# Output projection: the tail rows held in both row halves, with a ScalarE copy of the second tile's tail

## The chip, the cores and the metric

The kernel runs on one core of a Trainium2 chip. The metric is the time of one execution in microseconds of device time. A smaller number is better.

## The reference

Four layers are applied in turn to `x` of shape 1 x 2048 x 576: attention, gated unit, attention, gated unit. Each adds to `x` and starts with a layer norm. Both attention layers use the same weights, and so do both gated units.

```python
def _A_ref(x, wqkv, wo):                     # H = 32 heads of Dh = 18
    qkv = transpose((x @ wqkv).reshape(B, S, 3, H, Dh), 2, 0, 3, 1, 4)
    q, k, v = qkv[0], qkv[1], qkv[2]
    idx = pos[:, None] - (arange(8) * 2)[None, :]      # 8 positions, 2 apart
    ...
    attn = softmax(where(idx >= 0, q . kg * Dh ** -0.5, -1e9))
    o = sum over the window of attn * vg
    return o.transpose(0, 2, 1, 3).reshape(B, S, D) @ wo

def _B_ref(x, w_gate, w_up, w_down):         # F = 4608
    return ((x @ w_gate) * (x @ w_up)) @ w_down

x = x + _A_ref(_layernorm(x), A_wqkv, A_wo)
x = x + _B_ref(_layernorm(x), B_w_gate, B_w_up, B_w_down)
x = x + _A_ref(_layernorm(x), A_wqkv, A_wo)
x = x + _B_ref(_layernorm(x), B_w_gate, B_w_up, B_w_down)
```

The last step of the attention, `o @ wo`, is the output projection. The change is there.

## The kernel before, in words

The 2048 rows are cut into tiles of 128. A block `j` is an attention layer and a gated unit over one or two tiles (`nst` is 1 or 2). The first four blocks have one tile, the other 14 have two.

The width of 576 is four pieces of 128 (`KF` = 4) and a tail of 64 (`TL`). The attention keeps its result transposed in `oT`: 128 partitions, five pieces (the fifth, index `KF`, is the tail), and up to 256 columns, which are the rows of the block, 128 for each tile. In the tail piece the lower 64 partitions hold zeros. VectorE forms `oT` as a sum of eight products over the window (the first product at L772, the adds at L786). `wo_p` holds the weights in the same layout. Its tail fills partitions 0 to 63 (two DMAs, L392), and a memset on GpSimd (L341, part of `mk_zero`) puts zeros into partitions 64 to 127.

In blocks of one tile, the projection uses the whole array: five matmuls with 128 rows for each half of the output columns (L826).

In blocks of two tiles, the array is used as two halves of 64 rows which work side by side. `strip(i, r, hh, first)` is the list of matmuls of tile `i` on row half `r` (0 is partitions 0 to 63, 1 is 64 to 127) for output column half `hh` (288 columns). Row half 0 goes over five pieces and row half 1 over four, since the tail is only in the upper partitions. A tile's two column halves are summed in two PSUM banks, one of the `pg` and one of the `pu` family (`acct` and `pa` are the fourth of each). In a first pass half 0 works on the bank of the first column half while half 1 works on the other; in a second pass they swap. The order is: tile 0 first pass, tile 1 first pass, tile 0 second pass, tile 1 second pass. `both(a, b, fence)` issues two such lists in alternation, one matmul of each at a time. `fence` (L471) makes ScalarE copy one element, `tok`, from a bank when the tile's first pass is done; the first matmul of the second pass waits for that copy. When both passes are done, VectorE adds each bank to `xf` (`res`, L796), and this frees the bank.

The other users of TensorE in this scheme are `quarter` (L900, gate and up projections), `down2` (L968 and L969, down projection) and `project` (L527, query, key and value). They split their work over the two row halves in the same way, and their own tails are held for both halves.

The order of the work on each engine is not written out by hand. `Plan` is a planner that runs when the program is built: each `op` names an engine, an expected cost in ns, what it reads (`r`) and writes (`w`), and a priority. The planner gives each engine a list of instructions by its own estimate of start times, and the engines then go through these lists in order. An `op` may have a `margin`, which is added to the time when its inputs are ready: for the projection that is 500 ns in block 4 and 5 and 1200 ns after. The `tok` copies, the evacuations of gated units (L911 on ScalarE, L912 on VectorE) and `res` are marked as due, which puts them ahead of attention work that would delay them. So another cost or another dependence can change the order on every engine.

At the start, SP issues the loads in this order: rows of `x` and the query, key and value weights, then `wo_p`, then the gated unit's weights in six slices, with the first slabs of `w_down` between them.

Of the kernel before, what the change touches and what calls it, by code (L numbers as in the profile page):

```python
# [10 lines left out]
ACT = mybir.ActivationFunctionType  # L11
# [21 lines left out]
class Plan:  # L33
# [13 lines left out]
    def op(self, eng, cost, fn, r=(), w=(), prio=1, after=None, hold=None, free=None, margin=0, nbytes=0, use=None,  # L47
           pair=None, need=None, due=False, late=0, half=False):
        o = Op()
        o.rank, o.late, o.half = -1 if due else self.rank, late, half  # L50
        o.eng, o.cost, o.fn, o.prio, o.hold, o.free = eng, cost, fn, prio, hold, free
        o.margin, o.idx, o.succ, o.order, o.nbytes = margin, len(self.ops), [], set(), nbytes
        o.lat, o.use, o.pair, o.need = self.LAT[eng], use, pair, need
        d = set()
        for k in r:
            d.update(self.wr.get(k, ()))
        for k in w:
            d.update(self.wr.get(k, ()))
# [12 lines left out]
        o.n = len(d | o.order)  # L71
        self.ops.append(o)
        return o
# [96 lines left out]
def kernel(  # L170
# [12 lines left out]
    nc = tc.nc  # L183
    _, S, D = A_x.shape
    F = B_w_gate.shape[1]
    P = 128
    H, W, DIL = 32, 8, 2
    Dh = D // H
    HALO = (W - 1) * DIL
    KF = D // P  # L190
    TL = D - KF * P
    KT = KF + 1
# [6 lines left out]
    HD = D // 2  # L199
# [22 lines left out]
    wo_p = sb("wo_p", [P, KT, D])  # L222
# [21 lines left out]
    oT = sb("oT", [P, KT, CH])  # L244
    n_al = nlayers // 2
# [47 lines left out]
    def dma(dst, src):  # L293
        return lambda: nc.sync.dma_start(dst, src)
# [36 lines left out]
    def setup_b():  # L331
        def mk_zero():
            for t_ in qT_:
                nc.gpsimd.memset(t_[TL:P, KF, :], 0.0)
            for t_ in kv_:
                nc.gpsimd.memset(t_[TL:P, :, KF, :], 0.0)
            nc.gpsimd.memset(q_x[TL:P, KF, :], 0.0)
            nc.gpsimd.memset(kv_x[TL:P, :, KF, :], 0.0)
            for t_ in halo:
                nc.gpsimd.memset(t_[:], 0.0)  # L340
            nc.gpsimd.memset(wo_p[TL:P, KF, :], 0.0)  # L341
        op("POOL", 2600, mk_zero, w=[f"{x}{t}{i}" for x in "qkv" for t in (4, "H") for i in ZN] + [f"halo{i}" for i in range(n_al)] + ["wo_z"])
        for k in range(KT):
            def perm(eng, cost, key, t3, rk, k=k):
                if t3 < 3:
                    wr = wrawb[:, k, :] if t3 == 2 else wrawa[:, k, t3 * D:(t3 + 1) * D]
                    src = wr.rearrange("p (h d) -> p d h", h=H)[:, 0:16, :]
                    dst = wqkv[:, k, t3 * 512:(t3 + 1) * 512].rearrange("p (d h) -> p d h", h=H)
                else:
                    t0, t1 = (0, 2) if t3 == 3 else (2, 3)  # L350
                    src = (wrawa, wrawb)[t3 - 3][:, k, :].rearrange("p (t h d) -> p t d h", t=t1 - t0, h=H)[:, :, 16:18, :]
                    dst = wqkv[:, k, 3 * 512:3 * D].rearrange("p (t d h) -> p t d h", t=3, h=H)[:, t0:t1]
                fn = {"DVE": nc.vector.tensor_copy, "POOL": nc.gpsimd.tensor_copy, "ACT": nc.scalar.copy}[eng]
                pl.rank = 0.5
                op(eng, cost, lambda: fn(dst, src), r=rk, w=[key], prio=2 + (t3 in (2, 4)))  # L355
                pl.rank = 0
            ra, rb = [[f"wraw{c}{k}"] if k < KF else [f"wrawt{c}0", f"wrawt{c}{TL}"] for c in "ab"]
            perm("DVE", 530, f"wq0_{k}", 0, ra)
            perm("DVE", 180, f"wq3_{k}", 3, ra)
            if k % 2:  # L360
                perm("DVE", 530, f"wq1_{k}", 1, ra)
            else:
                perm("ACT", 1000, f"wq1_{k}", 1, ra)
            perm(VP[k], {"ACT": 1050, "DVE": 560, "POOL": 1250}[VP[k]], f"wq2_{k}", 2, rb)
            perm(VT[k], {"ACT": 330, "DVE": 200, "POOL": 300}[VT[k]], f"wq4_{k}", 4, rb)

        def mk_sel():
            nc.gpsimd.memset(Esel[:], 0.0)
            nc.gpsimd.memset(Bsel[:], 0.0)
            for j in range(4):  # L370
                nc.gpsimd.affine_select(out=Esel[:], in_=Esel[:], compare_op=ALU.not_equal,
                                        fill=1.0, base=-32 * j, pattern=[[-1, 32]], channel_multiplier=1)
                nc.gpsimd.affine_select(out=Bsel[:, j], in_=Bsel[:, j], compare_op=ALU.not_equal, fill=1.0,
                                        base=-32 * j, pattern=[[0, 4], [-1, 32]], channel_multiplier=1)
        op("POOL", 2900, mk_sel, w=["sel"], prio=3)

        def mk_cap():
            nc.gpsimd.memset(cap[:], 3e38)
            for i_ in range(W):
                if wlist[i_] > 0:  # L380
                    nc.gpsimd.memset(cap[:, i_, 0:DIL * wlist[i_]], -1e9)
        op("POOL", 1000, mk_cap, w=["cap"], prio=3.5)

        op("DVE", 0, lambda: None, r=[f"wq{t}_{k}" for t in (0, 1, 3) for k in range(KT)], w=["prod0", "prod1", "s10", "Lt"])
        op("ACT", 0, lambda: None, r=[f"wq{t}_{k}" for t in (2, 4) for k in range(KT)], w=["s11", "s12", "ab"])

    def setup_wo():
        wv_ = A_wo.rearrange("(h d) n -> h d n", d=Dh)
        for dd in range(4):
            op("SP", 470, dma(wo_p[32 * dd:32 * dd + 32, 0:KF, :], wv_[:, dd:16:4, :]), w=[f"wo{dd}"], nbytes=32 * KF * D * 2, prio=2.6)  # L390
        for dd in range(2):
            op("SP", 470, dma(wo_p[32 * dd:32 * dd + 32, KF, :], wv_[:, 16 + dd, :]), w=[f"wot{dd}"], nbytes=32 * D * 2, prio=2.6)  # L392

    def setup_glu():
        fw = F // FS
# [5 lines left out]
            op("SP", 550, dma(wgu_t[0:TL, fs], B_w_gate[KF * P:D, fs]), w=[f"wgt{s}"], nbytes=TL * fw * 2, prio=4 + s)  # L401
            op("SP", 550, dma(wgu_t[TL:2 * TL, fs], B_w_up[KF * P:D, fs]), w=[f"wut{s}"], nbytes=TL * fw * 2, prio=4 + s)

    wok = ["wo_z", "wot0", "wot1"] + [f"wo{dd}" for dd in range(4)]

    def head(src, keys, nst, dst, key, prio, ab, on_pe, mg, c0=0, halves=False):

# [56 lines left out]
    def both(a, b, fence=None):  # L464
        its = [f() for p in zip_longest(a, b) for f in p if f]
        if fence:
            tc.add_manual_dep(its[0].ins, fence["at"].ins.name, sync)

    def fence(box, src, keys):
        def fn():  # L470
            box["at"] = nc.scalar.copy(tok[0:1, :], src())  # L471
        op("ACT", 190, fn, r=keys, prio=0, due=True)
# [20 lines left out]
    def attention(j, la, t0, nst):  # L493
# [20 lines left out]
        def bank(p_, u):  # L514
            return (pg, pu)[p_][u["slot"]]
# [281 lines left out]
        if nst == 2:  # L797
            us = [{"left": 2}, {"left": 2}]
            fs = [{}, {}]
            o = None  # L800

            def strip(i, r, hh, first):
                def one(t):
                    rows = slice(TL * r, TL * r + TL)
                    return nc.tensor.matmul(bank(hh, us[i])[:, 0:HD], lhsT=oT[rows, t, i * P:(i + 1) * P], rhs=wo_p[rows, t, hh * HD:(hh + 1) * HD],  # L805
                                     start=(first and t == 0), stop=(not first and t >= KF - 1), skip_group_check=True)
                return [lambda t=t: one(t) for t in range(KF + 1 - r)]
            for first in (True, False):
                for i in range(nst):
                    kw = dict(pair=tuple(us), margin=mg) if o is None else dict(after=o, need=us[i])  # L810
                    o = op("PE", KT * TILE * HD, lambda i=i, first=first: both(strip(i, 0, 0 if first else 1, first), strip(i, 1, 1 if first else 0, first),
                                                                                           None if first else fs[i]),
                           r=["oT", "oTt", *wok], w=[f"wo{j}_{i}"], prio=0, half=True, **kw)
                    if first:
                        fence(fs[i], lambda i=i: bank(0, us[i])[0:1, 0:1], [f"wo{j}_{i}"])
            for i in range(nst):
                for hh in range(2):
                    op("DVE", 370, lambda i=i, hh=hh: res(bank(hh, us[i]), i, hh), r=[f"wo{j}_{i}", xin_k[i]], w=[fk[i], f"{fk[i]}h{hh}"] + guard,
                       prio=0, free="unit", use=us[i], due=True)
# [291 lines left out]
```

## Time and profile before

| | us |
|---|---|
| median of 3 runs (1056.66 to 1058.14) | 1057.23 |
| the profiled execution | 1056.22 |
| its span, first to last instruction | 1054.4 |
| TensorE busy (99%) | 1040.7 |
| VectorE busy (75%) | 786.2 |
| ScalarE busy (39%) | 410.8 |
| GpSimd busy (1%) | 8.9 |

The span is the part of the profiled execution between its first and its last instruction; 1.8 us lie around it. In the rows of the profile, PE is TensorE's matmuls, PEld its weight loads, DVE is VectorE, ACT is ScalarE, POOL is GpSimd and SP the queue that issues the DMAs. A group of instructions is given by line, engine, operation, output and inputs, shape and count, then busy time and the mean duration of one, then the idle time of the engine ahead of them and what ended it. Matmuls are pipelined, so the duration of one is longer than the distance between two starts.

### The profile page before, as it was taken

How to read it: one execution, taken by the hardware profiler on the slowest of the kernel's cores; microseconds unless marked ns; L12 is line 12 of the kernel's file. 1: busy time of each engine (PE TensorE's matmuls, PEld its weight loads, DVE VectorE, ACT ScalarE, POOL GpSimd, SP SyncE). 2: the span in 40 equal slices, each digit the busy share in tenths (PEclk: the TensorE clock that was granted, in tenths of full speed). 3: DMA queues.
4: the chain of work that ended last, by engine and by line, in shares of the span. 5: the costliest groups of instructions: out<-in, count | busy, mean ns of one | idle time of the engine just before them, and what ended most of it. 6: DMA issues, size and time to landing. Idle time of an engine off the chain costs nothing.

```text
span 1054.4 us, 39972 instructions
## 1 busy us (share of the span) xinstructions
PE 1040.7 (99%) x17845; PEld 829.9 (79%) x17863; DVE 786.2 (75%) x1477; ACT 410.8 (39%) x1090; POOL 8.9 (1%) x33
## 2 busy tenths in 40 slices
PE   7999999999999999999999999999999999999998
PEld 4888878787788898778887777877887788777776
DVE  7688989786979996979798876676878758833332
ACT  6752254343334544333434323334344252232221
POOL 3000000000000000000000000000000000000000
PEclk9999999999999999999999999999999999999999
DMA  9966563524262543254444534334353334343332
GB/s 272 317 186 194 177 185 104 155 63 145 69 149 81 146 105 107 70 149 128 120 93 107 140 114 118 93 115 95 93 151 82 99 90 126 116 135 96 116 101 69
DMA packets 146828, 133.68 MB, mean 127 GB/s; under 512 B 42272, under 2 KB 146016, under 8 KB 146656
## 3 DMA queue, kind: packets, MB, share of 16 engines
q1 hardware_dynamic: 146656, 131.13, 44.1%
q8 instruction: 139, 2.28, 0.9%
q14 instruction: 33, 0.27, 0.1%
HBM read 118.51 MB, written 4.06 MB: 116 GB/s over the span
## 4 chain that ended last, share of the span: by engine, by line
PE 82%; DVE 11%; DMA 4%; SPq 1%; issue 1%; ACT 1%; DVEq 0%; ACTq 0%
PE pg L900 15%; PE pu L900 14%; PE pu L968 9%; PE pg L968 8%; PE pa L900 5%; PE acct L900 5%; PE pg L527 4%; PE pu L527 3%; PE pu L876 3%; PE pg L876 3%; PE pg L928 2%; DVE scr L772 2%; DVE oT L786 2%; DMA scr<-a_dram 2%; DVE h L912 2%; PE pg L805 1%
## 5 line engine op out<-in xcount | busy, mean ns | idle before, releaser
L900 PE MATMUL pg<-xnT_B,wg 64*128 64x256 bf16 x3072 | 395.3, 269 | 0.5 <-DVE xf L796 0.5
L900 PE MATMUL pu<-xnT_B,wu 64*128 64x256 bf16 x3072 | 395.0, 269 | 0.5
L900 PEld LDWEIGHTS <-wg 64*128 64x128 bf16 x4032 | 367.7, 94 | 29.7 <-issue 2.6
L900 PEld LDWEIGHTS <-wu 64*128 64x128 bf16 x4032 | 366.8, 94 | 23.5 <-issue 0.6
L968 PE MATMUL pg<-wd,h 64*128 64x512 bf16 (+1 forms) x972 | 252.0, 377 | 0.8 <-DVE h L912 0.8
L968 PE MATMUL pu<-wd,h 64*128 64x512 bf16 (+1 forms) x971 | 252.1, 377 | 0.0
L912 DVE TENSOR_TENSOR h<-pu,g_sb 128x512 bf16<-128x512 f32 x228 | 153.5, 686 | 73.8 <-ACT g_sb L911 69.7
L968 PEld LDWEIGHTS <-h 64*128 64x128 bf16 (+1 forms) x1992 | 115.1, 94 | 100.3 <-DVE h L912 2.9
L911 ACT CAST g_sb<-pg 128x512 bf16<-128x512 f32 x228 | 132.1, 586 | 127.6 <-PE pg L900 91.6
L471 ACT COPY tok<-pu 1x1 f32<-1x1 f32 x254 | 37.4, 147 | 258.7 <-PE pu L900 191.8
L900 PE MATMUL acct<-xnT_B,wg 64*128 64x256 bf16 x960 | 130.7, 269 | 0.0
L900 PE MATMUL pa<-xnT_B,wu 64*128 64x256 bf16 x960 | 130.6, 269 | 0.0
L969 PEld LDWEIGHTS <-h 64*128 64x128 bf16 (+1 forms) x1992 | 114.1, 95 | 1.3 <-issue 0.6
L527 PEld LDWEIGHTS <-wqkv 64*128 64x128 bf16 (+1 forms) x2044 | 103.2, 94 | 15.0 <-issue 2.6
L900 PE MATMUL pg<-xnT_B,wgu_t 64*128 64x256 bf16 x384 | 103.3, 269 | 0.0
L900 PE MATMUL pu<-xnT_B,wgu_t 64*128 64x256 bf16 x384 | 103.3, 269 | 0.0
L969 PE MATMUL pa<-wd,h 64*128 64x64 bf16 (+1 forms) x540 | 102.1, 189 | 0.1
L969 PE MATMUL acct<-wd,h 64*128 64x64 bf16 (+1 forms) x540 | 102.1, 189 | 0.0
L697 DVE TENSOR_TENSOR scr<-qT,kv 128x1280 bf16<-128x1280 bf16 x104 | 82.4, 816 | 25.9 <-ACT kv L611 25.9
L786 DVE TENSOR_TENSOR oT<-oT,scr 128x1280 bf16<-128x1280 bf16 (+1 forms) x119 | 90.9, 764 | 3.2
L527 PE MATMUL pg<-xnT_A,wqkv 64*128 64x256 bf16 (+2 forms) x826 | 92.6, 260 | 0.5 <-ACT wqkv L355 0.3
L527 PE MATMUL pu<-xnT_A,wqkv 64*128 64x256 bf16 (+2 forms) x786 | 90.1, 262 | 0.8 <-DVE kv L609 0.4
(156 smaller groups left out, 1598.2 us busy)
## 6 DMA issues: line engine op xcount, KB each, us to landing
wd<-in_B_w_down_dram SPq DMA_DIRECT2D x324, 288.0 KB, 4.4
scr<-a_dram SPq DMA_DIRECT2D x52, 128.0 KB, 2.7
wg<-in_B_w_gate_dram SPq DMA_DIRECT2D x6, 768.0 KB, 10.0
wu<-in_B_w_up_dram SPq DMA_DIRECT2D x6, 768.0 KB, 11.3
out_dram<-xf SPq DMA_DIRECT2D x16, 144.0 KB, 3.0
xb<-in_A_x_dram SPq DMA_DIRECT2D x6, 288.0 KB, 2.9
a_dram<-scr SPq DMA_DIRECT2D x13, 128.0 KB, 2.4
scr<-in_A_wqkv_dram SPq DMA_DIRECT2D x4, 288.0 KB, 3.6
```

The costliest lines, as they stand in the source:

```text
L471: box["at"] = nc.scalar.copy(tok[0:1, :], src())
L527: return nc.tensor.matmul(bank(p_, u)[0:m, e * n:(e + 1) * n], lhsT=wqkv[r_, k, w0:w0 + m], rhs=xnT_A[r_, k, c0:c0 + n], start=start, stop ...
L697: op("DVE", 70 + 2.6 * n, lambda p_=p_, e=e: nc.vector.tensor_tensor(late["prod"][p_ % 2][:, e, :, 0:n], qT[:, :, 0:n], kT[:, :, HALO - DI ...
L772: nc.vector.tensor_tensor(js(dst), js(vT[:, :, o0:o0 + n]), abw, op=ALU.mult)
L786: op("DVE", 70 + 2.63 * n, lambda i_=i_: nc.vector.tensor_tensor(oT[:, :, 0:n], oT[:, :, 0:n], late["prod"][i_ % 2][:, 0, :, 0:n], op=ALU. ...
L876: nc.tensor.matmul(pt[:, e * n:(e + 1) * n], lhsT=w_[:, k, ft * P:(ft + 1) * P], rhs=xT[:, k, 0:n], start=(first and k == 0 and e == 0), s ...
L900: return nc.tensor.matmul(ps[:, e * n:(e + 1) * n], lhsT=w_, rhs=xT[rows, k, 0:n], start=(first and e == 0 and k == 0), stop=(not first an ...
L911: op("ACT", 490, lambda: nc.scalar.copy(g_sb[gs][:, 0:ul], pg[use["slot"]][:, 0:ul]), r=[f"wg_{j}_{u}"], w=[f"g{gs}"], prio=0, due=True)
L912: op("DVE", 605, lambda: nc.vector.tensor_tensor(hb[hs][:, 0:ul], pu[use["slot"]][:, 0:ul], g_sb[gs][:, 0:ul], op=ALU.mult), r=[f"wu_{j}_{ ...
L928: nc.tensor.matmul((pg, pu)[i][use["slot"]][:], lhsT=lhs, rhs=wt[:, e % 2, 0:512], start=first, stop=fin)
L968: return [lambda: nc.tensor.matmul((pg, pu)[i][use["slot"]][:], lhsT=lhs, rhs=wt[rows, e % 2, 0:512], start=first, stop=fin, skip_group_ch ...
L969: lambda: nc.tensor.matmul((pg, pu)[i][tl["slot"]][:, 0:TL], lhsT=lhs, rhs=wt[rows, e % 2, 512:D], start=first, stop=fin, skip_group_check ...
```

## The change

The tail of `wo` is loaded into both halves of `wo_p`'s tail piece, by four DMAs instead of two. The memset of the lower half goes. In blocks of two tiles, ScalarE copies the second tile's tail columns of `oT` from partitions 0 to 63 to partitions 64 to 127, and the matmul for the second tile's tail runs on row half 1; the first tile's stays on row half 0. For the second tile `both` begins with row half 1, and its fence reads the other bank. The planner's cost of a pass goes from 5 to 4.5 pieces.

```diff
@@ setup_b
-            nc.gpsimd.memset(wo_p[TL:P, KF, :], 0.0)
-        op("POOL", 2600, mk_zero, w=[...] + [f"halo{i}" for i in range(n_al)] + ["wo_z"])
+        op("POOL", 2600, mk_zero, w=[...] + [f"halo{i}" for i in range(n_al)])
@@ setup_wo
         for dd in range(2):
-            op("SP", 470, dma(wo_p[32 * dd:32 * dd + 32, KF, :], wv_[:, 16 + dd, :]), w=[f"wot{dd}"], nbytes=32 * D * 2, prio=2.6)
+            for r_ in (0, TL):
+                op("SP", 470, dma(wo_p[r_ + 32 * dd:r_ + 32 * dd + 32, KF, :], wv_[:, 16 + dd, :]), w=[f"wot{dd}{r_}"], nbytes=32 * D * 2, prio=2.6)
@@
-    wok = ["wo_z", "wot0", "wot1"] + [f"wo{dd}" for dd in range(4)]
+    wok = [f"wot{dd}{r_}" for dd in range(2) for r_ in (0, TL)] + [f"wo{dd}" for dd in range(4)]
@@ attention, nst == 2
-                return [lambda t=t: one(t) for t in range(KF + 1 - r)]
+                return [lambda t=t: one(t) for t in range(KF + (i == r))]
+            op("ACT", 280, lambda: nc.scalar.copy(oT[TL:P, KF, P:2 * P], oT[0:TL, KF, P:2 * P]), r=["oT"], w=["oTt"], prio=prio)
             for first in (True, False):
                 for i in range(nst):
                     kw = dict(pair=tuple(us), margin=mg) if o is None else dict(after=o, need=us[i])
-                    o = op("PE", KT * TILE * HD, lambda i=i, first=first: both(strip(i, 0, 0 if first else 1, first), strip(i, 1, 1 if first else 0, first),
-                                                                                           None if first else fs[i]),
+                    o = op("PE", (KF + 0.5) * TILE * HD, lambda i=i, first=first: both(*[strip(i, r, r if first else 1 - r, first) for r in (i, 1 - i)],
+                                                                                      None if first else fs[i]),
                            r=["oT", "oTt", *wok], w=[f"wo{j}_{i}"], prio=0, half=True, **kw)
                     if first:
-                        fence(fs[i], lambda i=i: bank(0, us[i])[0:1, 0:1], [f"wo{j}_{i}"])
+                        fence(fs[i], lambda i=i: bank(i, us[i])[0:1, 0:1], [f"wo{j}_{i}"])
```

More of the change, by code (lines that the diff above doesn't have):

```diff
@@ L340, in mk_zero @@
                 nc.gpsimd.memset(t_[:], 0.0)
-            nc.gpsimd.memset(wo_p[TL:P, KF, :], 0.0)
-        op("POOL", 2600, mk_zero, w=[f"{x}{t}{i}" for x in "qkv" for t in (4, "H") for i in ZN] + [f"halo{i}" for i in range(n_al)] + ["wo_z"])
+        op("POOL", 2600, mk_zero, w=[f"{x}{t}{i}" for x in "qkv" for t in (4, "H") for i in ZN] + [f"halo{i}" for i in range(n_al)])
         for k in range(KT):
```

## The prediction

> **What bounds the kernel now.** I read the page first, then TensorE's waits, then one output projection instruction by instruction, then the queues that the change touches.
>
> ```profile
> span 1054.4 us, 39972 instructions
> PE 1040.7 (99%) x17845; PEld 829.9 (79%) x17863; DVE 786.2 (75%) x1477; ACT 410.8 (39%) x1090; POOL 8.9 (1%) x33
> PEclk9999999999999999999999999999999999999999
> ```
>
> TensorE is busy 99% of the span at full granted clock. Its busy time is modelled, so I also added up the streaming time of every recorded matmul (columns by 0.4256 ns, half of it where two row halves run side by side): between 400 and 1050 us it fills 49 to 50 us of every 50. VectorE (75%) and ScalarE (39%) have room. The program is one long TensorE stream, and taking time out of that stream shortens the span, unless the next instruction then waits for something else. In TensorE's list of waits, after the start-up, almost nothing stands:
>
> ```profile
> PE pg L968 <- DVE h L912: 0.8, 3, 0.4
> PE pg L900 <- DVE xf L796: 0.5, 1, 0.5
> PE pu L969 <- DVE xf L796: 0.2, 1, 0.2
> ```
>
> Now one output projection (L805) in the timeline of TensorE; columns are start, duration, engine, line, operation, output and inputs.
>
> ```profile
> 482.75 0.28 PE L805 MATMUL pg<-wo_p,oT 64*128 64x288 bf16 x1
> 482.75 0.28 PE L805 MATMUL pu<-wo_p,oT 64*128 64x288 bf16 x1
> 482.87 0.28 PE L805 MATMUL pg<-wo_p,oT 64*128 64x288 bf16 x1
> ...
> 483.24 0.28 PE L805 MATMUL pg<-wo_p,oT 64*128 64x288 bf16 x1
> 483.25 0.28 PE L805 MATMUL pu<-wo_p,oT 64*128 64x288 bf16 x1
> 483.36 0.28 PE L805 MATMUL pg<-wo_p,oT 64*128 64x288 bf16 x1
> ...
> 484.94 0.27 PE L900 MATMUL pg<-xnT_B,wg 64*128 64x256 bf16 x1
> 484.96 0.28 PE L805 MATMUL pu<-wo_p,oT 64*128 64x288 bf16 x1
> 485.04 0.27 PE L900 MATMUL pg<-xnT_B,wg 64*128 64x256 bf16 x1
> 485.08 0.28 PE L805 MATMUL pu<-wo_p,oT 64*128 64x288 bf16 x1
> ...
> 485.20 0.27 PE L900 MATMUL pu<-xnT_B,wu 64*128 64x256 bf16 x1
> ```
>
> The two row halves of the array run in parallel, one on pg and one on pu, so 0.28 us of duration costs only the 0.1226 us pitch between two starts of the same half. The upper half (rows 0 to 63) has 5 matmuls in each of the four passes, 20 in all, and starts them without one gap from 482.75 to 485.08: 2.33 us over 19 steps is that pitch. The lower half has 16. It runs ahead (its first matmul of the second tile is the pu at 483.25, before the upper half's at 483.36) and begins the next operation at 484.94, when the upper half still has two to do and begins at 485.20. The upper half sets the time. Twelve of the 14 projections of this form have this shape to within 0.01 us.
>
> **The change, part by part.** *Four matmuls move.* The second tile's tail goes to the lower half: 5+4+4+5 = 18 in each half instead of 20 and 16; still 36. The upper half loses two pitches, 2 x 0.1226 = 0.245 us; 14 projections give 3.43 us. The lower half gains nothing: it leaves now 2.18 us after the start (484.94) and with 18 matmuls leaves at 18 x 0.1226 = 2.21. So a projection yields between -0.02 us, if what follows is paced by the lower half, and 0.245. I take 0.245, because the operations behind (L900, L968, L527) give both halves equal work, so the half that arrives last sets their end.
>
> The Trainium skill ("TensorE: Matmul & The Clock Gate", The mechanism) says that matmuls start and end strictly in program order. By that rule the lower half could not run ahead, every projection would give both halves the full 0.245 us, and the lower end of -0.02 would fall away; the sum stays 3.43. The rows at 483.25 and 483.36 contradict the rule here.
>
> *The bank hand-over.* Each tile's second pass swaps halves on the two banks and waits for ScalarE's one-element copy (`tok`, L471) of the first pass. In this block the last matmul of the second tile's first pass starts at 483.86, `tok` at 484.23, and the second pass at 484.44: 0.58 us. The time to hide it becomes five pitches, 0.613 us, for both tiles (first tile: upper half's 5th to its 10th matmul; second: the lower half's the same). That leaves 0.03 us. In 13 of 14 projections the first `tok` starts 0.81 to 0.87 us after the projection does, so ScalarE is free then. I take zero; at 0.05 us in each of 28 passes it would be 1.4 us.
>
> *ScalarE's copy, 64 x 128 bf16, 14 times.* The nearest rows are these:
>
> ```profile
> L656 ACT COPY halo<-kv 128x140 bf16<-128x140 bf16 x17 | 5.3, 309 | 0.4
> L638 ACT ACTIVATE qT<-pu 64x128 bf16<-64x128 f32 x4 | 1.1, 266 | 0.1
> L471 ACT COPY tok<-pg 1x1 f32<-1x1 f32 x21 | 3.1, 149 | 11.7 <-PE pg L805 11.5
> ```
>
> I take 0.30 us (SBUF to SBUF, 128 instead of 140 columns); 4.2 us on an engine that is idle 640. It stands on the way from VectorE's last add (L786) to TensorE. The projection now begins 0.36 us after that add in one block, 1.14 in the next, and 1.6 to 13.5 in the other twelve; and the planner counts the copy with 280 + 150 ns and keeps its margin behind it. Only the first block can be touched: 0 to 0.1 us. The copy is also a new wait in ScalarE's queue. Behind it stand `tok` copies and the evacuations L911, which let TensorE go on. If VectorE is finished when ScalarE gets there, it costs at most 0.30 us against a cover of half a microsecond (a pass of L900 is 10 x 0.109 = 1.09 us, the hand-over 0.58). I take 0.1 us in all.
>
> *Two more DMAs, one memset less.* SP issues the six `wo_p` loads at 10.5 to 13.3 us, about 0.43 us each with 4.6 us to landing; two more shift the weights of the gated unit by 0.9 us. The first of them is issued at 13.4, lands 10 us later, and L876 first reads it at 33.6; no wait of TensorE for a DMA is in its list. Cover 8 us or more: zero, at most 0.9 without it. The projection of the first block reads `wo_p` at 26.9, the new loads land by 19. POOL loses 0.57 us at 4.2 us; what follows it is needed at 13.2: zero.
>
> *What waits next.* Behind some projections TensorE needs a bank that VectorE's residual adds (L796) must free, and VectorE is then in other work:
>
> ```profile
> 533.21 0.82 DVE L697 TENSOR_TENSOR scr<-qT,kv 128x1280 bf16<-128x1280 bf16 x1
> 533.94 0.45 DVE L796 TENSOR_TENSOR xf<-pg,xb 128x288 f32<-128x288 f32 x1
> 534.31 0.45 DVE L796 TENSOR_TENSOR xf<-pu,xb 128x288 f32<-128x288 f32 x1
> 534.44 0.27 PE L900 MATMUL pg<-xnT_B,wg 64*128 64x256 bf16 x1
> 534.81 0.27 PE L900 MATMUL pu<-xnT_B,wu 64*128 64x256 bf16 x1
> ```
>
> L900 stands until the two adds are done, and those started when L697 let them, not when the projection ended. Such gaps follow five projections (at 216, 327, 377, 483 and 531 us; 2.2 us together). There the 0.245 us can vanish: 0 to 1.23 us lost. The planner writes a new order in which the adds may stand one VectorE instruction earlier or later, so I take the middle, 0.6.
>
> Sum: -3.43 + 0.6 + 0.1 = -2.7 us. The profiled execution took 1056.22 us (span 1054.4 and 1.8 around it), so 1053.5 by it; it lies 1.0 under the median of 1057.23, which gives 1054.5.
>
> **The rivals.** *VectorE takes over the wait (0.20).* If the gap behind the projection appears in nine blocks instead of five, 5 x 0.245 = 1.2 us is left: 1056.0. For it: VectorE is busy 87% of 200 to 600 us. Against: it is busy 71% of 600 to 800 us and 53% after that, and no such gap follows any of the last six projections.
>
> *ScalarE stands at the copy (0.15): slower.* If the order puts the copy where VectorE is still one pair of multiply and add behind (0.75 + 0.82 = 1.6 us), ScalarE stands 1.6 us, copies 0.3, and the hand-over or evacuation behind it loses 0.5 of cover: 1.4 us of TensorE per block. It decides from 2.5 blocks on (3.43 / 1.4); five blocks cost 7.0: 1060.8. For it: ScalarE works in order, and unlike TensorE it is given no margin. Against: TensorE's gaps behind the last add are mostly longer than the planned margin, so VectorE is not behind its plan there.
>
> *The lower half paces (0.05).* Then nothing is won: 1057.2 with a copy too many.
>
> **How the numbers follow.** The forecast case has 0.60. Its own range is 1052.8 (full 3.43 and 1.0 of the 2.2 us of gaps gone by the new order) to 1055.5 (all 1.23 us of the gaps' share lost, and 0.5 at ScalarE). For the first rival the range must reach 1057, and then into the slower one: up to three and a half blocks of it (3.5 x 1.4 - 3.43 = +1.5) is 1058.7, taken as 1059.0. About 0.10 stays above, 0.08 below. A difference under 0.2% (2.1 us) is about what a measurement of this kernel can't tell from none. Faster by more: most of the forecast case and a little of the first rival, 0.60; within it: the rest of that rival, the third, and the mild end of the second, 0.27; slower: 0.13.
>
> **What would show it.** Right: L805 still 504 matmuls, a projection from first start to the end of its stream 2.21 us instead of 2.45, both halves leaving within 0.05 us of each other; 14 copies of about 0.30 us; TensorE's granted clock unchanged. Wrong in size: gaps before L900 or L968 behind more than five projections, released by L796. Wrong in sign: idle time of ScalarE in front of the new copy released by L786, and TensorE gaps in front of a second pass. Wrong altogether: the time unchanged although each projection is 0.245 us shorter; then the lead of the lower half had been used.

## The result and the profile after

| | median us | runs |
|---|---|---|
| before | 1057.71 | 22, 1055.81 to 1058.78 |
| after | 1059.22 | 22, 1057.73 to 1060.91 |

The ratio is 1.0014, with an interval of 1.0008 to 1.002. The changed kernel is 1.5 us slower. That is under the 0.2% that the prediction calls hard to tell from none, but the interval leaves out 1. The forecast was 2.7 us the other way, and the median lies 0.2 us above the stated range. The profiled execution took 1059.04 us, 2.8 more than before's.

The head of the page of after, and the first line of its chain of waits, with the same line of before under it:

```profile
span 1057.3 us, 39948 instructions
PE 1038.0 (98%) x17845; PEld 835.9 (79%) x17863; DVE 786.1 (74%) x1477; ACT 414.6 (39%) x1104; POOL 8.3 (1%) x32
PEclk9999999999999999999999999999999999999999
PE 70%; DVE 22%; DMA 4%; ACT 1%; issue 1%; SPq 1%; POOL 0%; DVEq 0%; POOLq 0%; ACTq 0%
PE 82%; DVE 11%; DMA 4%; SPq 1%; issue 1%; ACT 1%; DVEq 0%; ACTq 0%
```

TensorE is busy for 2.7 us less and the span is 2.9 us longer, at the same granted clock. The chain that ended last runs through VectorE for 22% of the span; in before it was 11%. That share alone tells nothing of the time: in run 15 below, which is faster than both, it is 20%. The idle time has a place. These are rows of the busy time by stretch; the first two numbers are the length of the stretch and TensorE's busy time. First before, then after:

```profile
200.00:400.00 200.00, 198.10 (x3468) 163.91 (x3466) 173.55 (x319) 82.38 (x233) 0.00 (x0) 1.00 0.41 108
400.00:560.00 160.00, 159.86 (x2826) 127.23 (x2823) 137.75 (x248) 61.80 (x174) 0.00 (x0) 1.00 0.42 114
```

```profile
200.00:400.00 200.00, 195.93 (x3458) 169.47 (x3455) 171.82 (x316) 83.06 (x236) 0.00 (x0) 1.00 0.41 108
400.00:560.00 160.00, 158.25 (x2806) 129.20 (x2804) 137.51 (x245) 63.18 (x176) 0.00 (x0) 1.00 0.41 111
```

Between 200 and 560 us TensorE idles 5.82 us instead of 2.04. This is the stage in which VectorE is busiest (the third pair of numbers, 86% in both stretches). TensorE's list of waits after the start-up, in after:

```profile
PE pg L901 <- DVE xf L796: 2.5, 3, 1.1
PE pu L901 <- DVE h L913: 1.1, 1, 1.1
PE pu L970 <- DVE h L913: 1.1, 1, 1.1
```

From before's L808 on, after's line numbers are one higher, so L901 is before's L900. The wait of L901 for the residual adds was 0.5 us, once. Now it is 2.5 us, three times, and new waits for the evacuations of the gated unit stand beside it.

The same projection as the prediction shows, in the timeline of TensorE:

```profile
484.99 0.28 PE L805 MATMUL pg<-wo_p,oT 64*128 64x288 bf16 x1
485.00 0.28 PE L805 MATMUL pu<-wo_p,oT 64*128 64x288 bf16 x1
...
485.97 0.28 PE L805 MATMUL pg<-wo_p,oT 64*128 64x288 bf16 x1
485.98 0.28 PE L805 MATMUL pu<-wo_p,oT 64*128 64x288 bf16 x1
486.10 0.27 PE L901 MATMUL pa<-xnT_B,wu 64*128 64x256 bf16 x1
486.11 0.27 PE L901 MATMUL acct<-xnT_B,wg 64*128 64x256 bf16 x1
...
486.86 0.27 PE L901 MATMUL pa<-xnT_B,wu 64*128 64x256 bf16 x1
486.97 0.28 PE L805 MATMUL pu<-wo_p,oT 64*128 64x288 bf16 x1
...
487.95 0.28 PE L805 MATMUL pu<-wo_p,oT 64*128 64x288 bf16 x1
487.96 0.28 PE L805 MATMUL pg<-wo_p,oT 64*128 64x288 bf16 x1
488.07 0.38 PE L969 MATMUL pg<-wd,h 64*128 64x512 bf16 x1
```

Both halves have nine matmuls from 484.99 and nine from 486.97, and leave together at 488.07: 2 x 9 x 0.1226 = 2.21 us of own time, as predicted. But eight pairs of L901 (part of `quarter`) now stand between the first passes and the second: 0.87 us. The projection's banks are held for 3.08 us instead of 2.45. In after, other matmuls stand there in all 14 projections: eight pairs in ten of them, two pairs of the down projection (0.25 us) in three, and two matmuls of a block of one tile in the first (0.45 us). In before, they stand there in one.

One of TensorE's longest waits in this stretch comes in the next block, whose projection has two pairs between its passes. The timeline of all engines there:

```profile
536.59 0.19 PE L970 MATMUL pu<-wd,h 64*128 64x64 bf16 x1
536.66 0.82 DVE L697 TENSOR_TENSOR scr<-qT,kv 128x1280 bf16<-128x1280 bf16 x1
536.87 0.15 ACT L471 COPY tok<-pu 1x1 f32<-1x1 f32 x1 [1.46 <-PE pu L970]
537.39 0.45 DVE L796 TENSOR_TENSOR xf<-pg,xb 128x288 f32<-128x288 f32 x1
537.76 0.45 DVE L796 TENSOR_TENSOR xf<-pu,xb 128x288 f32<-128x288 f32 x1
537.90 0.27 PE L901 MATMUL pg<-xnT_B,wg 64*128 64x256 bf16 x1 [1.12 <-DVE xf L796]
538.26 0.27 PE L901 MATMUL pu<-xnT_B,wu 64*128 64x256 bf16 x1
```

TensorE has run out of work that needs no bank of the projection. The adds came too late, VectorE took an attention product (L697) first, and the matmul started at 536.59 is followed by the next at 537.90. That this wait comes from the gap between the passes is not shown by these rows alone; the experiments below test it.

### The profile page after: what moved, and what is told of

It reads as the page before. It is cut to its first block, busy times and chain, and to the rows that moved or that the text cites. A ratio compares the mean times of both kernels' runs of the same rounds, so it can differ in the third digit from the quotient of the medians.

```text
span 1057.3 us, 39948 instructions
## 1 busy us (share of the span) xinstructions
PE 1038.0 (98%) x17845; PEld 835.9 (79%) x17863; DVE 786.1 (74%) x1477; ACT 414.6 (39%) x1104; POOL 8.3 (1%) x32
## 4 chain that ended last, share of the span: by engine, by line
PE 70%; DVE 22%; DMA 4%; ACT 1%; issue 1%; SPq 1%; POOL 0%; DVEq 0%; POOLq 0%; ACTq 0%
PE pg L901 14%; PE pu L901 12%; PE acct L969 4%; PE pa L969 4%; DVE oT L786 4%; DVE scr L772 4%; PE acct L901 4%; PE pa L901 4%; PE pg L969 4%; PE pu L969 4%; DVE h L913 3%; PE pu L877 3%; PE pg L527 3%; PE pg L877 3%; DVE scr L697 3%; PE pu L527 2%
## 5 line engine op out<-in xcount | busy, mean ns | idle before, releaser
L901 PE MATMUL pg<-xnT_B,wg 64*128 64x256 bf16 x3088 | 400.1, 269 | 2.5 <-DVE xf L796 2.5
L901 PE MATMUL pu<-xnT_B,wu 64*128 64x256 bf16 x3088 | 399.2, 269 | 1.4 <-DVE h L913 1.1
L901 PEld LDWEIGHTS <-wg 64*128 64x128 bf16 x4032 | 371.4, 94 | 28.9 <-issue 4.1
L901 PEld LDWEIGHTS <-wu 64*128 64x128 bf16 x4032 | 372.9, 94 | 22.4 <-issue 2.8
L969 PEld LDWEIGHTS <-h 64*128 64x128 bf16 (+1 forms) x1992 | 111.2, 94 | 100.7 <-issue 2.4
L970 PE MATMUL pu<-wd,h 64*128 64x64 bf16 (+1 forms) x852 | 161.1, 189 | 1.1 <-DVE h L913 1.1
L970 PE MATMUL pg<-wd,h 64*128 64x64 bf16 (+1 forms) x852 | 161.1, 189 | 0.1
L471 ACT COPY tok<-pu 1x1 f32<-1x1 f32 x283 | 41.7, 147 | 296.7 <-PE pu L901 199.5
L969 PE MATMUL pg<-wd,h 64*128 64x512 bf16 x552 | 143.1, 377 | 0.6 <-DVE h L913 0.6
L969 PE MATMUL pu<-wd,h 64*128 64x512 bf16 x552 | 143.1, 377 | 0.0
L901 PE MATMUL pa<-xnT_B,wu 64*128 64x256 bf16 x944 | 128.4, 269 | 0.8 <-DVE h L913 0.8
L901 PE MATMUL acct<-xnT_B,wg 64*128 64x256 bf16 x944 | 129.0, 269 | 0.0
L969 PE MATMUL acct<-wd,h 64*128 64x512 bf16 (+1 forms) x444 | 114.8, 377 | 0.0
L969 PE MATMUL pa<-wd,h 64*128 64x512 bf16 (+1 forms) x443 | 114.8, 377 | 0.0
L970 PEld LDWEIGHTS <-h 64*128 64x128 bf16 (+1 forms) x1992 | 112.3, 95 | 1.3 <-issue 0.4
L901 PE MATMUL pg<-xnT_B,wgu_t 64*128 64x256 bf16 x386 | 103.8, 269 | 0.0
L901 PE MATMUL pu<-xnT_B,wgu_t 64*128 64x256 bf16 x386 | 103.8, 269 | 0.0
L697 DVE TENSOR_TENSOR scr<-qT,kv 128x1280 bf16<-128x1280 bf16 x104 | 82.0, 816 | 16.5 <-ACT kv L611 16.5
```

Of the source, the lines that this page charges most:

```text
L697: op("DVE", 70 + 2.6 * n, lambda p_=p_, e=e: nc.vector.tensor_tensor(late["prod"][p_ % 2][:, e, :, 0:n], qT[:, :, 0:n], kT[:, :, HALO - DI ...
L901: return nc.tensor.matmul(ps[:, e * n:(e + 1) * n], lhsT=w_, rhs=xT[rows, k, 0:n], start=(first and e == 0 and k == 0), stop=(not first an ...
L969: return [lambda: nc.tensor.matmul((pg, pu)[i][use["slot"]][:], lhsT=lhs, rhs=wt[rows, e % 2, 0:512], start=first, stop=fin, skip_group_ch ...
L970: lambda: nc.tensor.matmul((pg, pu)[i][tl["slot"]][:, 0:TL], lhsT=lhs, rhs=wt[rows, e % 2, 512:D], start=first, stop=fin, skip_group_check ...
```

## Experiments

Three theories stood at the beginning. **A: the plan's gap.** The planner counts a pass as 4.5 x 0.4265 x 288 = 553 ns now and 614 before. It counts the hand-over (TensorE's latency 250, `tok` 190, ScalarE's latency 150) as 590 ns. Before, the second pass was ready in the plan when the first passes ended; now it is 37 ns late, and the planner puts another operation in between. On the chip the hand-over takes 0.58 us and would have fitted in 0.613. **B: the copy.** ScalarE's new copy waits for the last add, and what is queued behind it is late. **C: the start.** The two more DMAs cost about 0.9 us there. C can be answered at once: the first evacuation of the gated unit (`h`) stands at 37.97 to 39.51 us in the traces with the new loads, and at 38.25 to 39.14 us in those without, so no cost shows.

All ratios below are to before in runs beside it, with the 95% interval.

**1. The old cost, all else as in after.**

```diff
-  o = op("PE", (KF + 0.5) * TILE * HD, lambda ...
+  o = op("PE", KT * TILE * HD, lambda ...
```

> The changed kernel with one number put back: the planner's cost of a projection pass is 5 pieces (614 ns) as before, though the pass has 4.5. Theory A (the planner): with 4.5 pieces (553 ns) the second pass isn't due yet by the plan when the first pass of the other tile ends, because the plan counts 250 + 190 + 150 = 590 ns for the hand-over by tok; so the plan puts other matmuls in between, the banks are held longer, and TensorE waits for them afterwards. By A the second pass now follows at once in 13 of 14 projections, the gaps behind the projections fall from 8.3 us back to about 2.2, and the 3.4 us show: 1054 to 1055.5 us. Theory B (the ScalarE copy lengthens the way to the projection and delays the order): nothing changes, 1058.5 to 1059.5. Theory C (the two more DMAs at the start cost 0.9 us and more): at most 1 us of the 3.4 is missing.

1059.60 us, 1.0011 [1.0000, 1.0022]. The gap is gone in 12 of 14 projections, and the time is not back. A alone fails. B's number (1058.5 to 1059.5) is missed by 0.1 us, beside a before whose median stood 0.9 us higher here than in the result.

**2. The new cost in the kernel before**, nothing else.

```diff
-  o = op("PE", KT * TILE * HD, lambda ...
+  o = op("PE", (KF + 0.5) * TILE * HD, lambda ...
```

> The kernel before with one number of the change: the planner's cost of a pass is 4.5 pieces, while the array work stays 20 and 16 matmuls in the halves, without copy and with the old loads. A: other matmuls slip between the passes in all 14 projections and the time rises by the excess gaps, 4 to 6 us: 1062 to 1064. B, C, and the theory that the order is chance: within 1 us of before, 1057 to 1058.5.

1060.64 us, 1.0018 [1.0008, 1.0028], with matmuls between the passes in all 14. No work changes here, only a number in the plan. This fits A at half the size that I had put on it. But the order on all engines is a new one too, and what that does by itself is asked in runs 13 and 14.

**3. A shorter `tok` in the plan** (150 instead of 190 for the projection's two; the plan's hand-over becomes 550, under 553).

```diff
-        op("ACT", 190, fn, r=keys, prio=0, due=True)
+        op("ACT", cost, fn, r=keys, prio=0, due=True)     # 150 from the projection
```

> The changed kernel with the planner's cost of the projection's tok copies at 150 ns instead of 190 (measured: 148), the pass kept at 4.5 pieces. By the plan the hand-over is then 550 ns, 3 less than a pass. A: the second pass follows at once, as in the kernel with the pass cost put back, 1054 to 1056 us; the order of later blocks differs, so up to 1 us more or less. B: as the changed kernel, 1058.5 to 1059.5.

1057.17 us, 0.9986 [0.9976, 0.9996]: faster, and 1.2 us above A's number. One projection of 14 has the gap. This kernel has the copy on ScalarE, as run 1 has, and is faster than before. ScalarE stands in front of the copy nearly as long as in after (9.4 us, nine times), so that standing need not cost anything: it depends on what the order puts behind the copy. This speaks for A and against B, and run 1 the other way; the next runs take the parts singly.

**4. Run 1 without the copy** (which leaves the tail of each second tile out of the result).

```diff
-  op("ACT", 280, lambda: nc.scalar.copy(oT[TL:P, KF, P:2 * P], oT[0:TL, KF, P:2 * P]), ...)
```

> The changed kernel with the pass cost at 5 pieces and without ScalarE's copy; this leaves out the tail of each second tile (the lower half holds zeros there). Its order on TensorE is that of the kernel before, instruction for instruction, with 18 and 18 matmuls in the halves. So it shows the balance alone: A: 14 x 0.245 = 3.4 us less the share lost in gaps, 1054 to 1055. The theory that the lower half paces: 1057.5. The difference to the kernel with copy and pass cost 5 is the cost of the copy: A says 0 to 0.5 us, B 2 us or more.

1056.86 us, 0.9983 [0.9974, 0.9991]. Apart from the moved matmuls and their loads, and the 14 `tok` copies that read the other bank, TensorE, VectorE and ScalarE have before's instructions in before's order. This is the balance alone, and it gives 1.7 us instead of 3.43 (0.9 to 2.8 by the interval).

**5. The copy alone, in the kernel before** (nothing reads what it writes).

```diff
+  op("ACT", 280, lambda: nc.scalar.copy(oT[TL:P, KF, P:2 * P], oT[0:TL, KF, P:2 * P]), ...)
```

> The kernel before with ScalarE's copy alone: it is made, the projection waits for it in the plan, and nothing reads what it writes; 20 and 16 matmuls in the halves. Its order on TensorE is that of the changed kernel with pass cost 5. Theory B (the copy costs: ScalarE stands at it until VectorE's last add, the evacuations behind it come late, VectorE takes other work first, and the adds that free the banks come late): 2 to 2.7 us slower than before, most of it in one or two blocks. Theory A alone (only the pass cost of the plan matters): as before, within 0.5 us.

1060.17 us, 1.0020 [1.0012, 1.0029]. The order is that of run 1, not that of before. So the 1.9 us are the price of the copy together with the order that the planner writes for it; its own work is 4.2 us on an engine that is idle for 640.

Where it costs shows in run 1 at the block of 533 us. The timeline of ScalarE and VectorE there:

```profile
529.58 0.82 DVE L786 TENSOR_TENSOR oT<-oT,scr 128x1280 bf16<-128x1280 bf16 x1
529.63 0.31 ACT L512 COPY kv<-halo 128x140 bf16<-128x140 bf16 x1 [0.93 <-DVE scr L772]
530.32 1.55 DVE L697 TENSOR_TENSOR scr<-qT,kv 128x1280 bf16<-128x1280 bf16 x2
530.44 0.30 ACT L808 COPY oT<-oT 64x128 bf16<-64x128 bf16 x1 [0.49 <-DVE oT L786]
530.76 0.59 ACT L912 CAST g_sb<-pg 128x512 bf16<-128x512 f32 x1
...
532.53 0.39 PE L969 MATMUL pg<-wd,h 64*128 64x512 bf16 x1 [0.54 <-DVE h L913]
```

And in before, the same instructions:

```profile
528.27 0.82 DVE L786 TENSOR_TENSOR oT<-oT,scr 128x1280 bf16<-128x1280 bf16 x1
528.33 0.31 ACT L512 COPY kv<-halo 128x140 bf16<-128x140 bf16 x1 [0.55 <-DVE scr L772]
528.54 0.58 ACT L911 CAST g_sb<-pg 128x512 bf16<-128x512 f32 x1
```

In before, the evacuation (`g_sb`) starts 0.27 us after the last add starts. In run 1 ScalarE stands 0.49 us for that add, copies for 0.30, and starts the evacuation 1.18 us after it: 0.9 us later. Then `h` is late, L969 waits for it, VectorE's work shifts, the residual adds of this block start at 536.70, and L901 waits 1.21 us for them. Measured by the successive evacuations `h`, runs 1 and 5 both lose 1.8 us against before in this one block (523 to 550 us). Run 4, with the same projection and no copy, loses none there, and neither does run 6 below. The block is not all: the traced execution of run 5 is 3.9 us behind that of before at the end (before's lies 1.5 us under its median). Over the whole of after, ScalarE stands in front of the copy for 10.6 us, in nine of 14 blocks. Its row among the groups:

```profile
L808 ACT COPY oT<-oT 64x128 bf16<-64x128 bf16 x14 | 4.1, 296 | 10.8 <-DVE oT L786 10.6
```

**6. Run 1 with the copy on GpSimd**, which has nothing else to do after the start.

```diff
-  op("ACT", 280, lambda: nc.scalar.copy(...
+  op("POOL", 280, lambda: nc.gpsimd.tensor_copy(...
```

> The changed kernel with pass cost 5 and the copy on GpSimd instead of ScalarE, with the same cost in the plan. GpSimd has nothing else to do by then, so nobody stands behind the copy. B: ScalarE's evacuations are on time again and the time falls to that of the kernel without a copy, 1056.5 to 1057.3 (1.5 us under before). If instead the longer way to the projection is what costs (the 430 ns that the plan adds), it stays at 1059 to 1060.

1057.41 us, 0.9985 [0.9975, 0.9995]: as good as no copy at all. At the same block:

```profile
531.42 0.82 DVE L786 TENSOR_TENSOR oT<-oT,scr 128x1280 bf16<-128x1280 bf16 x1
531.47 0.31 ACT L512 COPY kv<-halo 128x140 bf16<-128x140 bf16 x1 [0.80 <-DVE scr L772]
531.68 0.58 ACT L912 CAST g_sb<-pg 128x512 bf16<-128x512 f32 x1
...
532.40 0.73 POOL L808 COPY oT<-oT 64x128 bf16<-64x128 bf16 x1 [49.84 <-DVE oT L786]
```

The evacuation starts 0.26 us after the last add starts, as in before. The copy takes 0.73 us instead of 0.30, and nobody is queued behind it. The 12 executions of this run spread from 1054.14 to 1058.09. The order behind the copy is not run 1's everywhere, but at this place nothing else is seen to differ: it is not the copy's work that costs here, but what ScalarE holds up while it waits.

**7 and 8. VectorE out of the way.** In blocks of two tiles the last two of eight products and adds are left out (L772 and L786), with the plan's costs unchanged: in the kernel before (7), and in run 4 (8).

```diff
+                if nst == 2 and i_ in (6, 7):      # the product
+                    return
-  op("DVE", 70 + 2.63 * n, lambda i_=i_: nc.vector.tensor_tensor(oT[:, :, 0:n], ...
+  op("DVE", 70 + 2.63 * n, lambda i_=i_: None if nst == 2 and i_ in (6, 7) else nc.vector.tensor_tensor(oT[:, :, 0:n], ...
```

> The kernel before, with the last two of the eight products and adds over the window left out in the blocks of two tiles (the plan counts them as before, so every order is kept). VectorE loses 3.2 us in each of 14 blocks. By the theory that VectorE sets the pace between 190 and 540 us, the gaps of TensorE there (some 5 us) shrink: 1053 to 1056. If VectorE doesn't bind, no change: 1058.

> The balanced projection without copy (pass cost 5; the second tiles' tails left out) with the same two products and adds left out. Its difference to the kernel before with the same left out is the balance alone with VectorE out of the way: 3.4 us if VectorE had been taking up half of it, 1.7 us as without this if the missing half went elsewhere.

1053.34 us (0.9951 [0.9939, 0.9963]) and 1049.89 us (0.9919 [0.9905, 0.9932]). The orders are the same on these three engines, so the difference is the balance: 3.45 us, where the prediction worked out 3.43. With five executions of each, spread over 1.7 us, the agreement to 0.02 us is luck; an estimate by resampling these times gives 1.9 to 4.5 us. Within that, the gain is whole when VectorE has slack, and half of it when VectorE has not. TensorE's idle time between 200 and 560 us says the same. The rows of busy time by stretch of run 4, then of 7, then of 8:

```profile
200.00:400.00 200.00, 197.43 (x3472) 163.57 (x3468) 173.93 (x320) 82.63 (x233) 0.00 (x0) 1.00 0.40 108
400.00:560.00 160.00, 159.28 (x2810) 127.30 (x2806) 137.33 (x247) 61.03 (x172) 0.00 (x0) 1.00 0.41 113
```

```profile
200.00:400.00 200.00, 198.40 (x3504) 163.68 (x3500) 163.90 (x305) 84.59 (x236) 0.00 (x0) 1.00 0.40 108
400.00:560.00 160.00, 160.00 (x2839) 126.99 (x2836) 129.15 (x236) 61.07 (x172) 0.00 (x0) 1.00 0.42 116
```

```profile
200.00:400.00 200.00, 199.26 (x3534) 171.63 (x3532) 165.17 (x307) 85.67 (x238) 0.00 (x0) 1.00 0.41 109
400.00:560.00 160.00, 160.00 (x2850) 124.27 (x2848) 128.26 (x234) 61.22 (x172) 0.00 (x0) 1.00 0.43 117
```

TensorE idles 1.60 us in run 7 and 0.74 in run 8, but 2.04 in before and 3.29 in run 4. So in run 4 some 1.25 us of the gain came back as waiting, and in run 8 none.

**9. After, with the same edit.**

> The changed kernel as it is (pass cost 4.5, ScalarE's copy), with the last two of eight products and adds over the window left out in the blocks of two tiles, plan unchanged. If the slipped-in matmuls and the copy cost time only through VectorE, which frees the banks late, then nearly all of the balance shows against the kernel before with the same left out (1053.3): 1050 to 1051. If they cost TensorE time of their own, 1053 to 1055.

1052.86 us, 0.9944 [0.9931, 0.9958]. Missed: this is 3 us slower than run 8. This would mean that the gap and the copy cost even where VectorE has slack; but the orders of runs 8 and 9 differ, so the 3 us are not theirs for sure.

**10. After with the copy on GpSimd** (the gap without ScalarE's wait).

```diff
-  op("ACT", 280, lambda: nc.scalar.copy(...
+  op("POOL", 280, lambda: nc.gpsimd.tensor_copy(...
```

> The changed kernel with pass cost 4.5 as it is and the copy on GpSimd. Against the kernel with GpSimd's copy and pass cost 5 (0.15% under before) it shows what the slipped-in matmuls cost: as in the kernel before with pass cost 4.5, 2 us: 1059 to 1060. If they cost nothing beside the balance, 1057 to 1057.7.

1059.42 us, 1.0013 [1.0004, 1.0022]; 13 of 14 projections have the gap. In one stretch the plan's new cost has the same price whichever engine copies: measured by the evacuations `h` from 504 to 542 us, around the block shown above, after, run 10 and run 2 (which has no copy) lose 1.4, 1.4 and 1.5 us against before, and run 4 loses 0.1. With run 6 this gives the table of the balanced kernels:

| | copy on ScalarE | no copy | copy on GpSimd |
|---|---|---|---|
| second pass follows at once (cost 5) | 1.0011 | 0.9983 | 0.9985 |
| gap between the passes (cost 4.5) | 1.0014 (after) | | 1.0013 |

The kernels with either one have lost the gain and a little more. Together the two are no worse than one. It would fit if both use up the same slack, namely how late a bank of the projection may come free before TensorE needs it; no run shows that by itself.

**11 and 12. Getting rid of the last gaps.** Run 6 with the projection's margin smaller by 430 ns (11: no gap in any projection), and run 3's `tok` with the copy on GpSimd and that margin, at cost 4.5 (12).

```diff
-  kw = dict(pair=tuple(us), margin=mg) if o is None else ...
+  kw = dict(pair=tuple(us), margin=mg - 430) if o is None else ...
```

> A version meant to be better: pass cost 5, the copy on GpSimd, and the margin of the projection in the plan cut by the 430 ns that the copy adds there, so that the projections stand where they stood and no other matmul comes between the passes in any of the 14. By the theories A and B together: like the kernel without a copy, 0.17% under before, 1056 to 1057; at best 1055 if the new order has fewer gaps behind the projections.

> The same with the true pass cost (4.5) and tok at 150 ns in the plan instead of pass cost 5. One projection of 14 has matmuls between its passes. A and B: 1056 to 1057, like the version with pass cost 5; what lies between the two is the chance of the order.

1059.00 us, 1.0002 [0.9993, 1.0010], and 1057.22 us, 0.9992 [0.9983, 1.0001]. Run 11 has neither the gap nor ScalarE's wait for the copy, and no gain: missed. Another margin is another order on every engine.

**13 and 14. What another order is worth by itself**: the kernel before, with only the margin `mg` changed, by +430 ns (13) and by -430 ns (14).

```diff
-  kw = dict(pair=tuple(us), margin=mg) if o is None else ...
+  kw = dict(pair=tuple(us), margin=mg + 430) if o is None else ...      # 14: mg - 430
```

> The kernel before with one number of the plan changed and no work: the projection's margin is 430 ns longer (what the copy adds in the changed kernel). One projection of 14 gets other matmuls between its passes, and later blocks stand elsewhere. If the order alone moves the time by chance: anywhere from 1056.5 to 1060.5. If the extra 430 ns on the way in the plan is a cost of its own (part of what was put down to the copy): 1060 to 1061, like the kernel before with ScalarE's copy. If neither: within 0.5 us of before.

> The same with the margin 430 ns shorter, again without any change of work. Chance of the order: 1056.5 to 1060.5; otherwise within 0.5 us of before. With the one above it gives the size of what an order can do.

1061.26 us, 1.0020 [1.0011, 1.0029], and 1059.24 us, 1.0007 [0.9998, 1.0016]. No work was added or taken away. So a new order may cost 0.2% by itself, as much as anything in the table. Run 13 also lands 0.3 us above the number (1060 to 1061) that was expected if the 430 ns on the way in the plan were a cost of their own. Run 6 has the same 430 ns in its plan and is faster than before, so they need not cost; but how much of run 5's 1.9 us is the copy and how much this delay can't be told from the times. Where two kernels have different orders, their times alone don't tell which of the differences did it. The readings that stand without this are the pairs of one order (before and run 4, runs 1 and 5, runs 7 and 8) and the waits seen in the traces. Between runs 1 and 5 the balance changes the ratio from 1.0020 to 1.0011, but these two were measured beside different runs of before.

**15. Both causes taken away, with the projection's margin as it was**: after's cost of 4.5, run 3's `tok` of 150, run 6's copy on GpSimd.

```diff
-  op("ACT", 280, lambda: nc.scalar.copy(...
+  op("POOL", 280, lambda: nc.gpsimd.tensor_copy(...
-  op("ACT", 190, fn, r=keys, prio=0, due=True)
+  op("ACT", cost, fn, r=keys, prio=0, due=True)     # 150 from the projection
```

> The changed kernel with tok at 150 ns in the plan for the projection (so that the true pass cost of 4.5 pieces brings no other matmuls between the passes, in 13 of 14) and the copy on GpSimd: both causes taken away. A and B: 1055.5 to 1057, at least as good as either alone (1057.2 and 1057.4). If only chance of the order told these two from before: 1057 to 1060.

1055.79 us (1054.39 to 1056.43), 0.9968 [0.9956, 0.9980]. That is the gain of the forecast, and better than both kernels, but part of it is luck of the order: run 12 differs from this one only in the margin and has 0.9992, and the four kernels with the copy on GpSimd and at most two gaps (6, 11, 12, 15) lie between 0.9968 and 1.0002. TensorE idles 3.57 us between 200 and 560 us. The wait of L901 for the residual adds in this trace:

```profile
PE pg L901 <- DVE xf L796: 0.7, 1, 0.7
```

It is once 0.7 us, against three times and 2.5 us in after.

**16. The copy later in ScalarE's order**: run 1 with a margin of `mg - 200` on the copy, and 200 on the projection.

```diff
-  op("ACT", 280, lambda: nc.scalar.copy(...), r=["oT"], w=["oTt"], prio=prio)
+  op("ACT", 280, lambda: nc.scalar.copy(...), r=["oT"], w=["oTt"], prio=prio, margin=mg - 200)
-  kw = dict(pair=tuple(us), margin=mg) if o is None else ...
+  kw = dict(pair=tuple(us), margin=200) if o is None else ...
```

> The changed kernel with pass cost 5 and ScalarE's copy planned 1000 ns later than VectorE's last add (300 in the first two blocks), the projection's own margin cut by as much. ScalarE then should not stand at the copy waiting for VectorE. If standing there is what the copy costs: no idle time of ScalarE ahead of the copy, 1056.5 to 1058. If the copy costs in another way: 1059 to 1060. Three projections of 14 have other matmuls between their passes, which may add up to 0.5.

1058.56 us, 0.9998 [0.9989, 1.0006]. ScalarE stands in front of the copy five times for 5.0 us, instead of eleven times for 10.3 in run 1, and a tenth of a per cent comes back. Three of 14 projections have the gap, so this run leans toward B and no more.

## Why the prediction was wrong

**Right: the balance.** 504 matmuls, 18 pitches in each half, both halves leaving within 0.01 us of each other, and about 3.4 us for all of it where VectorE has room (3.45 between runs 7 and 8). The rival in which the lower half paces is out.

**Right: the hand-over on the chip.** Where the plan lets the second pass follow at once, it does so without a hole. In run 1 at the block of 533 us, starts of L805 follow each other at 0.12 us through both passes. The new loads and the missing memset show up in no time that can be told from before's: one wait of the start-up (L452) is for GpSimd instead of ScalarE, 1.2 us instead of 1.1. A few projections have a hole of 0.1 to 0.3 us ahead of the second tile's first pass, where a bank comes free late.

**The step that failed most: the plan.** "The planner writes a new order in which the adds may stand one VectorE instruction earlier or later." This was counted with 0.6 us and taken as chance. It wasn't: the prediction had the pass (five pitches, 0.613 us, on the chip) and compared it with the hand-over on the chip (0.58). The planner decides by its own numbers, 553 against 590, and those were in the code. Hence other matmuls between the passes of each of the 14 projections, 0.87 us of them in ten. That number alone, with the order that comes of it, made the kernel before slower by 0.18% (run 2).

**A term of the sum that was mis-sized: the copy.** "I take 0.1 us in all." The copies took 296 ns as predicted. With the order that came of them they cost 1.9 us (run 5). The trace shows 1.8 us lost in one block, where ScalarE stood at the copy; runs 4 and 6 lose none there. The reason given was "if VectorE is finished when ScalarE gets there"; it was not so in nine of 14 blocks. The slower rival had the mechanism right: ScalarE works in order, has no margin, and an evacuation stood behind the copy. It got the price right too, 1.4 us per block against 1.8 in that one, but not how often it is needed: it decides "from 2.5 blocks on", against the full 3.43. Of that, the next point had already taken half, so little more than one such block could use up the rest.

**A term that was too small: what VectorE takes back.** 0.6 us was taken, in a range of 0 to 1.23. With before's very order it was 1.7 (run 4: 3.43 of gain, 1.7 left). The gaps of run 4 follow the same five projections as before's; they grew longer, and TensorE's idle time between 200 and 560 us rose by 1.25 us, the upper end of that term. The remaining 0.5 us is within the spread of the times. The first rival, gaps behind more projections than five, is what after has: there TensorE stands behind eight projections for about 8 us, counted by the distances between starts, against 2.2 us behind five in before.

Together: 3.43 of gain, 1.7 given back with nothing else changed, and some 3 more by the plan's gap, the copy and the order that they brought. That is 1.5 us slower by the medians. How the 3 divide between the two can't be said, as they don't add. What part of it is this order's own chance stays open too: runs 11, 13 and 14 show that chance to be as large as 0.2%.

## What to carry to other kernels

Where a planner orders the work, a cost that is changed is part of the change: put the new number beside the plan's own latencies before anything else, since a pass that becomes 37 ns too short for the planned hand-over lets another operation in.

A copy on an engine that works in order can cost what stands behind it while it waits for its input, and not its 0.3 us; here an idle engine was the better place in the block that shows it, even at more than twice the duration. And where a new order by itself moves the time by 0.2%, compare kernels of one order, or the same block in several kernels.

When work leaves the bound engine, look stage by stage at who frees its buffers: here about half the gain went where VectorE was 86% busy, and came back when VectorE had less to do.

## What was not expected of the hardware

GpSimd's copy of 64 x 128 took either 0.29 or 0.73 us. Of the 13 in run 6 behind 200 us, seven took 0.73 (all of those up to 582 us but one) and six 0.29. Four rows of the timeline of run 6, two of each kind:

```profile
427.93 0.68 DVE L913 TENSOR_TENSOR h<-pa,g_sb 128x512 bf16<-128x512 f32 x1
428.17 0.29 POOL L808 COPY oT<-oT 64x128 bf16<-64x128 bf16 x1 [50.23 <-DVE oT L786]
...
481.58 1.65 DVE L697 TENSOR_TENSOR scr<-qT,kv 128x1280 bf16<-128x1280 bf16 x2
481.82 0.73 POOL L808 COPY oT<-oT 64x128 bf16<-64x128 bf16 x1 [53.36 <-DVE oT L786]
```

Beside an evacuation out of PSUM the copy is short. Beside a product of two tensors in SBUF it is long. The product that it starts beside keeps its usual time (0.82), but a second product that starts while the copy still runs takes 0.91, so the pair takes 1.65 here against 1.55 in run 1. The Trainium skill ("GPSIMD Engine Reference", 1. Specifications) says that GpSimd's way to SBUF is shared with VectorE, and that instructions of VectorE with two SBUF inputs contend for it. The rows agree, and so do all five runs with the copy on GpSimd: each of the 33 copies beside a product L697 took 0.73, and each of the other 37 took 0.29. The 23 products that started beside a running copy took 0.91, and the other 537 took 0.77 to 0.83.

The start differs from one execution to another. The first evacuation `h` in the kernel before with another margin stood at 38.29 us (run 13) and 38.82 (run 14), at 39.14 in run 2, and at 38.25 in before. So nearly 1 us of a difference between two single executions can come from ahead of anything that was changed.
